# Chunk 1 transposed by a DMA, with the work around it put at other hooks

## The chip, the cores and the metric

The kernel runs on one core of a Trainium2 chip. TensorE (PE) multiplies matrices, VectorE (DVE) and ScalarE (ACT) work elementwise, GpSimd (POOL) does small work and issues transfers, and SyncE (SP) only issues transfers. Each engine runs its own list of instructions in order and waits on semaphores for others. The metric is the device time of one execution in microseconds; lower is better. Before the change the median of five runs is 179.16 us (178.99 to 180.62).

## The reference, cut to what matters

```python
def _A_ref(x, w_r, w_i):                       # x: 1 x 2048 x 512
    X = rfft2(x.astype(float32), axes=(-2, -1))
    X = X * (w_r + 1j * w_i)                   # filter: 2048 x 257
    return irfft2(X, s=(S, D), axes=(-2, -1)).astype(bfloat16)

def _B_ref(x, w_gate, w_up, w_down):           # 512 -> 1792 -> 512
    h = gelu(x @ w_gate) * (x @ w_up)
    return h @ w_down

xn = layernorm(A_x)                            # over the last axis
out = A_x + _A_ref(xn, A_w_r, A_w_i) + _B_ref(xn, B_w_gate, B_w_up, B_w_down)
```

One row-wise normalized input goes to two branches, a two-dimensional Fourier filter and a gated feed-forward, whose results are added to the input. `B_x` is not read.

## The kernel before, in words

The 2048 rows are 16 tiles of 128 rows, taken as four chunks (m or b = 0 to 3) of four tiles. A chunk is normalized (`ln_stat`, `ln_aggr`, `ln_norm`: VectorE, with one reciprocal root on GpSimd) into a buffer `xn` or, for chunk 2, `tw`, and must then be transposed into `xnT`, features on partitions, because TensorE sums over partitions. `trans` does this with eight TensorE transposes into PSUM and one eviction, on VectorE or ScalarE, for half a chunk; `trans_dma` does a whole chunk with one transposing DMA from SyncE's queue. Chunks 0 and 1 use `trans` (chunk 0 partly in a finer form), chunks 2 and 3 `trans_dma`.

**Feed-forward.** For each chunk and each of 14 slices fc of the hidden size, `gate` and `up` are four matmuls each into one PSUM bank; ScalarE takes the gelu of the gate into one of three buffers and VectorE multiplies (L912). The second matmul of a chunk is done by `product`, a Strassen-like scheme: seven steps of seven matmuls for each pair of tiles, with sums of hidden slices (`sum_01`, `sums_S`) and of weights (`sums_T`) made on VectorE. Steps 0 and 3 of a product have ScalarE copy one PSUM bank to another (`copy`, L811); steps 2 and 4 add to those copies. The down weights `wd` come in four loads.

**Fourier branch.** Four stages. `butter` (VectorE, two parts per chunk) folds `xnT`, `unit_D` (one per tile) does the transform over features, `units_A` the first half of the transform over rows, and its result goes to DRAM scratch with `load_tv` reading it back in another order into `tv`. `unit_B` (eight, g = 0 to 7, needing all of `tv`) does the second half; VectorE multiplies by filter slice g (L606, `mul`); `unit_C` begins the inverse and writes to a second scratch, which `load_vv` reads back; `unit_E` and `unit_F` end the inverse and a GpSimd-issued accumulating DMA adds it to the result. The filter arrives in eight slices (`load_W`), each as eight loads: four for the real part by GpSimd's queue, four for the imaginary part by SyncE's, into a ring of four slots. `keep_256` copies a slice's last column, and `mini` (steps 0 to 4) takes that column's own path.

**Order.** It is written out by hand. The main loop runs over chunks b and slices n: `gate`, a hook, sometimes a product step (which has its own hook at its end), `up`, a hook. `hook` has a running number and emits what `at(number, ...)` has planned for it, in the order in which it was planned. So a hook number is a place in TensorE's instruction list, 0.86 us of matmuls or one product step from the next, and at the same time a place in every other engine's list: an operation planned at a hook stands behind all that was emitted before it on its engine. Hooks 0 to 27 lie in chunk 0's loop, from 28 in chunk 1's, from 69 in chunk 2's. `load_late` (L348) also waits until TensorE has reached the place where it was planned. Some work (`mul`, the feed-forward product) is put off to the end of the same hook by `later`.

SyncE's queue is the one the change orders anew: x and weight loads at the start, then scratch writes, transposing DMAs, scratch reads, the imaginary filter loads, and the output. The places are set in L960 to L1024.

Of the kernel before, what the change touches and what calls it, by code (L numbers as in the profile page):

```python
# [214 lines left out]
def bass_parallel_sum__spectral_gfnet__glu_gated_geglu__prompt_kernel(  # L215
# [27 lines left out]
    with ExitStack() as es:  # L243
# [328 lines left out]

        def load_W(s):
            hs = slice(2 * s, 2 * s + 2)
            for k, src in enumerate((A_w_r, A_w_i)):
                v = src.rearrange("(k2 r c h) k -> c k2 r h k", r=2, c=2, h=16)
                for c in range(2):
                    for i in range(2):
                        p0 = 64 * c + 32 * i
                        yield (load_late, W[k][s % 4][p0:p0 + 32, :, :, 0:KW], v[c][:, :, hs, :], [("W", k, s, c, i)], [("Wf", s % 4, k, c, i)], "sp" if k else "pool")  # L580
# [6 lines left out]
        def unit_B(g):  # L587
# [12 lines left out]
            i = g % 2  # L600
# [3 lines left out]
            def mul():  # L604
                for k in range(2):
                    op("dve", lambda e, k=k: e.tensor_tensor(pp[i][k], xc[i], W[k][g % 4][:, :, :, 0:256], ALU.mult),  # L606
                       r=[("xc", i)] + [key for c in range(2) for ii in range(2) for key in (("W", k, g, c, ii), ("Wf", g % 4, k, c, ii))], w=[("pp", i, k)])
# [338 lines left out]
        def at(h, *calls):  # L946
            plan.setdefault(int(h), []).extend(calls)
# [12 lines left out]
        for i in range(4):  # L960
            f0, f1 = (0, 4, 8, 11, 14)[i:i + 2]
            at(10 + 2 * i, (load_late, wd_sb[:, f0:f1, :], wdv[:, f0:f1, :], [("wd", fc) for fc in range(f0, f1)]))
        at(18, (load_late, be[:], c_be.ap(), ["be"]))
        at(19, (load_late, mm[:], c_mm.ap(), ["mm"]))
        for s, h0 in enumerate((30, 37, 49, 54, 61, 66, 70, 75)):
            for i, t in enumerate(load_W(s)):
                at(h0 + i // 2, t)
            at(89 + s // 2 if s > 3 else (47, 48, 57, 58)[s], (keep_256, s))
# [5 lines left out]
        for m in range(1, 4):  # L974
            a = (5, 15, 22)[m - 1]
            n = (10, 20, 27)[m - 1]
            t = (16, 29, 35)[m - 1]
# [5 lines left out]
            if m < 2:  # L983
                at(t, (trans, m, (0, 1), (0, 1, 2, 3)))
                at(t + 1, (trans, m, (2, 3), (0, 1, 2, 3), "act"))
            else:
                at(n + 1, (trans_dma, m))
# [4 lines left out]
        for m in range(4):  # L992
            h = (11, 22, 35, 40)[m]
# [5 lines left out]
            at(h + 8 + (4 if m < 1 else 0), (load_tv, m))  # L999
        for g in range(9):  # L1000
            h = int(59 + 4.6 * g)
# [17 lines left out]
        for k in range(4):  # L1019
            at((40, 43, 45, 47)[k], (sums_T, k))  # L1020
# [126 lines left out]
```

## Time and profile before

| What | Value |
|---|---|
| median of five runs | 179.16 us |
| the profiled execution: its own time, its span | 179.21 us, 177.4 us |
| TensorE busy | 171.9 us (97%) |
| VectorE, ScalarE, GpSimd busy | 132.4, 93.3, 54.8 us |
| granted TensorE clock | full in all slices |
| transfers | 27.89 MB, mean 157 GB/s |
| `gate` and `up` matmuls (L890, L906) | 58.1 and 57.9 us |
| TensorE's transposes of chunk 1 (L422) | two groups of eight, at 24.51 and 25.82 us |

The span is what the profiler recorded, the own time what the device measured; 1.8 us lie outside the span. Times in the text are us from the span's start. Matmuls are pipelined, so a row's length overlaps the next row's start; the distance between starts is what a group costs. Releasers of waits are inferred from semaphores.

### The profile page before, as it was taken

To read this page: it belongs to the slowest core of one execution; us is meant where nothing else is said; L and a number is where in the kernel's file an instruction comes from. 1 tells how busy PE (TensorE), PEld (TensorE's weight loads), DVE (VectorE), ACT (ScalarE), POOL (GpSimd) and SP (SyncE) were. 2 spreads that over 40 slices of the span, in tenths; PEclk is the share of its full clock that TensorE was granted. 3 is DMA by queue.
4 is the path that set the end of the run, shared out by engine and by line. 5 is a ranking of instruction groups with operands and counts; after the bars stand their busy time and mean duration, and the time that the engine had idled before them with its cause. 6 is when DMAs were issued, how large, how long until landed. Compare 5 with 4: busy or idle time off the path is not lost.

```text
span 177.4 us, 3787 instructions
## 1 busy us (share of the span) xinstructions
PE 171.9 (97%) x1394; PEld 107.3 (60%) x1394; DVE 132.4 (75%) x329; ACT 93.3 (53%) x156; POOL 54.8 (31%) x107
## 2 busy tenths in 40 slices
PE   7889999999999999999999999999999999999992
PEld 2477564554566566566565656566767666656881
DVE  2768899986588876867875749897867777897552
ACT  3343447764578523456656665337678576642110
POOL 2210444125041056194880000011544635530000
PEclk9999999999999999999999999999999999999999
DMA  4999999898998579479892204490165736551104
GB/s 118 294 237 308 285 291 307 249 206 222 200 179 164 145 199 220 94 197 209 206 240 49 85 20 122 125 328 25 31 118 106 137 86 118 92 91 30 30 6 118
DMA packets 31059, 27.89 MB, mean 157 GB/s; under 512 B 7120, under 2 KB 27984, under 8 KB 30912
## 3 DMA queue, kind: packets, MB, share of 16 engines
q1 hardware_dynamic: 25936, 19.75, 44.8%
q0 software_dynamic: 4272, 7.24, 19.2%
q10 hardware_dynamic: 832, 0.66, 1.4%
q8 instruction: 11, 0.18, 0.5%
q14 instruction: 8, 0.07, 0.2%
HBM read 18.19 MB, written 6.29 MB: 138 GB/s over the span
## 4 chain that ended last, share of the span: by engine, by line
PE 90%; DMA 4%; SPq 2%; ACT 1%; issue 0%; DVE 0%
PE ps L906 27%; PE ps L890 26%; PE ps L792 24%; DMA wu<-in_B_w_up_dram 4%; SPq L346 2%; PE ps L648 2%; PE ps L846 2%; PE ps L620 2%; PE ps L595 2%; PE ps L495 1%; PE ps L466 1%; PE ps L498 1%; PE ps L467 1%; ACT early L601 1%; PE ps L463 1%; ACT early L625 1%
## 5 line engine op out<-in xcount | busy, mean ns | idle before, releaser
L906 PE MATMUL ps<-xnT,wu 128*128 128x512 f16 (+1 forms) x240 | 57.9, 365 | 0.5 <-DMA wu<-in_B_w_up_dram 0.5
L890 PE MATMUL ps<-xnT,wg 128*128 128x512 f16 (+2 forms) x244 | 58.1, 362 | 0.2 <-DMA wg<-in_B_w_gate_dram 0.2
L912 DVE TENSOR_TENSOR hT<-ps,gl 128x512 bf16<-128x512 f32 (+1 forms) x60 | 39.0, 652 | 21.6 <-PE ps L906 15.4
L894 ACT ACTIVATE gl<-ps 128x512 bf16<-128x512 f32 (+1 forms) x60 | 34.1, 569 | 38.7 <-PE ps L890 37.6
L906 PEld LDWEIGHTS ps<-xnT,wu 128*128 128x128 bf16 x240 | 22.5, 98 | 20.6 <-DMA wu<-in_B_w_up_dram 0.6
L890 PEld LDWEIGHTS ps<-xnT,wg 128*128 128x128 bf16 x244 | 22.8, 98 | 16.0 <-issue 0.8
L349 POOL DMA_DIRECT2D wring<-in_A_w_r_dram x32 | 18.7, 661 | 14.2 <-PE ps L792 4.9
L657 POOL COPY tv<-tv 1x128 bf16<-1x128 bf16 x16 | 5.4, 338 | 40.4 <-ACT tv L655 40.3
L792 PE MATMUL ps<-wd,hT 128*128 128x256 bf16 x112 | 14.4, 273 | 0.0
L872 POOL DMA_DIRECT2D x_sb<-tv x16 | 13.2, 864 | 3.4 <-DVE tv L865 2.4
L606 DVE TENSOR_TENSOR early<-early,wring 128x1024 bf16<-128x1024 f16 x16 | 10.3, 687 | 3.7 <-ACT early L601 3.7
L811 ACT ACTIVATE ps<-ps 128x256 f32<-128x256 f32 x16 | 5.9, 372 | 12.9 <-PE ps L792 12.8
L393 DVE BATCH_NORM_STATS2 st<-x_sb 128x6 f32<-128x512 bf16 x16 | 10.6, 683 | 2.4 <-DMA x_sb<-in_A_x_dram 2.4
L401 POOL TENSOR_TENSOR rstd<-vpe,mhalf 128x4 f32<-128x4 f32 (+2 forms) x6 | 5.0, 836 | 23.5 <-DVE vpe L400 23.5
L792 PEld LDWEIGHTS ps<-wd,hT 128*128 128x128 bf16 x112 | 10.7, 98 | 2.5
L471 ACT ACTIVATE early<-ps 128x512 f16<-128x512 f32 x16 | 9.5, 597 | 4.2 <-PE ps L467 4.2
L852 ACT ACTIVATE tv<-ps 128x512 bf16<-128x512 f32 x16 | 9.5, 595 | 3.6 <-PE ps L846 3.6
L792 PE MATMUL ps<-arena,xnT 128*128 128x256 f16 x91 | 11.4, 273 | 0.0
L655 ACT ACTIVATE tv<-ps 128x512 bf16<-128x512 f32 x16 | 9.5, 595 | 3.2 <-PE ps L648 3.2
L601 ACT ACTIVATE early<-ps 128x1024 f16<-128x1024 f32 x8 | 8.2, 1022 | 4.9 <-PE ps L595 4.3
L792 PEld LDWEIGHTS ps<-arena,xnT 128*128 128x128 f16 x91 | 8.6, 98 | 2.3 <-DVE tw L815 0.3
L675 DVE TENSOR_TENSOR x_sb<-ps,x_sb 128x256 bf16<-128x256 f32 x16 | 6.7, 421 | 3.1 <-PE ps L792 3.0
(119 smaller groups left out, 237.4 us busy)
## 6 DMA issues: line engine op xcount, KB each, us to landing
wring<-in_A_w_r_dram POOLq DMA_DIRECT2D x32, 64.2 KB, 5.0
wring<-in_A_w_i_dram SPq DMA_DIRECT2D x32, 64.2 KB, 4.9
tv<-scr SPq DMA_DIRECT2D x8, 256.0 KB, 4.0
scr<-early SPq DMA_DIRECT2D x8, 256.0 KB, 3.0
wring<-scr SPq DMA_DIRECT2D x4, 512.0 KB, 6.0
x_sb<-tv POOLq DMA_DIRECT2D x16, 128.0 KB, 2.7
scr<-early SPq DMA_DIRECT2D x15, 128.0 KB, 3.6
out_dram<-x_sb SPq DMA_DIRECT2D x28, 64.0 KB, 2.1
```

The lines of the kernel that those rows point to most:

```text
L349: op(eng, lambda e: e.dma_start(dst, src), w=list(keys) + list(also), dma=True, after=[("pe", pr.cnt["pe"])])
L393: op("dve", lambda e: e.bn_stats(st[:, j, :], x_sb[:, j, :]), r=[("x", j, 0), ("x", j, 1)], w=[("st", j)])
L471: op("act", lambda e: e.activation(x4.rearrange("p (a c r) -> p a c r", a=2, r=4), bank(bk).rearrange("p (a r c) -> p a c r", a=2, r=4), A ...
L601: op("act", lambda e: e.activation(xc[i].rearrange("p r hh c -> p (r hh c)"), pair(bk), ACT.Copy, scale=SC_B), r=[("ps", bk), ("ps", bk + ...
L606: op("dve", lambda e, k=k: e.tensor_tensor(pp[i][k], xc[i], W[k][g % 4][:, :, :, 0:256], ALU.mult), r=[("xc", i)] + [key for c in range(2) ...
L655: op("act", lambda e: e.activation(z, bank(bk).rearrange("p (a c) -> p a c", a=4), ACT.Copy, scale=SC_E), r=[("ps", bk)], w=[zk] + (TVK if ...
L792: ins = e.matmul(o, st_(f), mv(f), start=(f == 0 and step in (0, 5)), stop=(f == 6), skip_group_check=True)
L872: op("pool", lambda e: e.dma_start(x_sb[:, j, :], ys, accum_op=ALU.add), r=[yk + (0,), yk + (1,), ("x", j, 0), ("x", j, 1)] + acc(j), w=ac ...
L890: ins = e.matmul(bank(bg)[:, c], wg_sb[:, dc, fc * P:(fc + 1) * P], xnT[:, j1:j1 + len(h), dc, :], start=(dc == 0), stop=(dc == 3), skip_g ...
L894: op("act", lambda e: e.activation(gl[k % 3][:, 0:n], bank(bg)[:, 0:n], ACT.Gelu_apprx_tanh), r=[("ps", bg)], w=[("gl", k % 3)])
L906: ins = e.matmul(bank(bu)[:, 0:n], wu_sb[:, dc, fc * P:(fc + 1) * P], xnT[:, j0:j0 + len(jjs), dc, :], start=(dc == 0), stop=(dc == 3))
L912: op("dve", lambda e: e.tensor_tensor(hT[b % 2][:, fc, h0:h0 + n], bank(bu)[:, 0:n], gl[k % 3][:, 0:n], ALU.mult), r=[("ps", bu), ("gl", k ...
```

## The change

Chunk 1 is transposed by `trans_dma`, at hook 11, instead of by two `trans` groups at hooks 16 and 17; its butterflies, `unit_D` and `units_A` stand three hooks later. The four loads of `wd` go from GpSimd's queue at hooks 10 to 16 to SyncE's at 13 to 16. `units_A` of chunks 1, 2 and 3 go to hooks 30, 38 and 44 (from 27, 40 and 45), the scratch reads of chunks 1 to 3 to 33, 45 and 47 (from 30, 43 and 48). Filter loads, `keep_256`, `unit_B`, `unit_C` and one `sums_T` get other hooks. `load_slice` only asserts while the program is built that a ring slot's earlier slice has been multiplied.

```diff
@@ -570,6 +570,12 @@
                 op("act", lambda e: e.activation(row[:], bank(bk)[96:128, 0:64], ACT.Copy, scale=SC_E), r=[("ps", bk)], w=["row"])
                 dma("sp", z256[0:1, :].rearrange("o (r q) -> o r q", q=64), row[:], r=["row"], w=["z256"] + TVK)
 
+        multiplied = set()
+
+        def load_slice(s, *t):
+            assert s < 4 or s - 4 in multiplied
+            t[0](*t[1:])
+
         def load_W(s):
             hs = slice(2 * s, 2 * s + 2)
             for k, src in enumerate((A_w_r, A_w_i)):
@@ -602,6 +608,7 @@
                r=[("ps", bk), ("ps", bk + 1)], w=[("xc", i)] + (EKEYS if g == 0 else []))
 
             def mul():
+                multiplied.add(g)
                 for k in range(2):
                     op("dve", lambda e, k=k: e.tensor_tensor(pp[i][k], xc[i], W[k][g % 4][:, :, :, 0:256], ALU.mult),
                        r=[("xc", i)] + [key for c in range(2) for ii in range(2) for key in (("W", k, g, c, ii), ("Wf", g % 4, k, c, ii))], w=[("pp", i, k)])
@@ -959,13 +966,13 @@
 
         for i in range(4):
             f0, f1 = (0, 4, 8, 11, 14)[i:i + 2]
-            at(10 + 2 * i, (load_late, wd_sb[:, f0:f1, :], wdv[:, f0:f1, :], [("wd", fc) for fc in range(f0, f1)]))
+            at(13 + i, (load_late, wd_sb[:, f0:f1, :], wdv[:, f0:f1, :], [("wd", fc) for fc in range(f0, f1)], (), "sp"))
         at(18, (load_late, be[:], c_be.ap(), ["be"]))
         at(19, (load_late, mm[:], c_mm.ap(), ["mm"]))
-        for s, h0 in enumerate((30, 37, 49, 54, 61, 66, 70, 75)):
+        for s, h0 in enumerate((31, 35, 50, 54, 63, 67, 72, 76)):
             for i, t in enumerate(load_W(s)):
-                at(h0 + i // 2, t)
-            at(89 + s // 2 if s > 3 else (47, 48, 57, 58)[s], (keep_256, s))
+                at(h0 + i // 2, (load_slice, s) + t)
+            at(89 + s // 2 if s > 3 else (46, 48, 60, 64)[s], (keep_256, s))
         cmv = c_cm.ap().rearrange("p (h r c) -> p h r c", h=NJ, r=2)
         for i, h0 in enumerate((54, 57, 63, 68)):
             hs = slice(4 * i, 4 * i + 4)
@@ -974,31 +981,27 @@
         for m in range(1, 4):
             a = (5, 15, 22)[m - 1]
             n = (10, 20, 27)[m - 1]
-            t = (16, 29, 35)[m - 1]
+            t = (19, 28, 35)[m - 1]
             for i in range(4):
                 at(a + i, (ln_stat, 4 * m + i))
             at(a + 3, (ln_aggr, 4 * m, 4))
             for i in range(4):
                 at(n + i // 2, (ln_norm, 4 * m + i))
-            if m < 2:
-                at(t, (trans, m, (0, 1), (0, 1, 2, 3)))
-                at(t + 1, (trans, m, (2, 3), (0, 1, 2, 3), "act"))
-            else:
-                at(n + 1, (trans_dma, m))
+            at(n + 1, (trans_dma, m))
             at(t + 2, (butter, m, 0))
             at(t + 3, (butter, m, 1))
         at(3, (butter, 0, 0))
         at(4, (butter, 0, 1))
         for m in range(4):
-            h = (11, 22, 35, 40)[m]
+            h = (11, 25, 33, 39)[m]
             for i in range(4):
                 at(h + i + (i if m < 1 else 0), (unit_D, 4 * m + i))
             at(h + 5 + (4 if m < 1 else 0), (units_A, m))
             if m == 3:
                 at(h + 7, (mini, 0))
-            at(h + 8 + (4 if m < 1 else 0), (load_tv, m))
+            at((23, 33, 45, 47)[m], (load_tv, m))
         for g in range(9):
-            h = int(59 + 4.6 * g)
+            h = int(60 + 4.5 * g)
             if g < 8:
                 at(h, (unit_B, g))
             if g > 0:
@@ -1017,7 +1020,7 @@
         for k in range(3):
             at((38, 39, 40)[k], (sum_01, 0, 0, k))
         for k in range(4):
-            at((40, 43, 45, 47)[k], (sums_T, k))
+            at((40, 43, 45, 46)[k], (sums_T, k))
         for k in range(4):
             at((101, 101, 102, 103)[k], (sums_S, 2, 0, 4, (k,)))
             at((106, 106, 107, 107)[k], (sums_S, 2, 4, 6, (k,)))
```

## The prediction, made before the changed kernel was run

> **What bounds the kernel now.** I read the page first: busy shares, then the chain that ended last.
>
> ```profile
> PE 171.9 (97%) x1394; PEld 107.3 (60%) x1394; DVE 132.4 (75%) x329; ACT 93.3 (53%) x156; POOL 54.8 (31%) x107
> ...
> PE 90%; DMA 4%; SPq 2%; ACT 1%; issue 0%; DVE 0%
> ```
>
> TensorE is busy 97% of the span, and the chain is TensorE's own work from 11.8 us (the first `up` of chunk 0, held by a weight load) to 174.2 us. So TensorE's instruction list is the time: an instruction removed there is worth its spacing, and a new wait there costs its length. Next, TensorE's rows in order of time where the change removes work:
>
> ```profile
> 23.65 1.03 PE L890 MATMUL ps<-xnT,wg 128*128 128x512 f16 x4
> 24.51 0.61 PE L422 MATMUL ps<-ident,cmx 128*128 128x128 f16 x8
> 24.96 1.03 PE L906 MATMUL ps<-xnT,wu 128*128 128x512 f16 x4
> 25.82 0.61 PE L422 MATMUL ps<-ident,cmx 128*128 128x128 f16 x8
> 26.27 0.22 PE L463 MATMUL ps<-fd,arena 128*128 128x128 f16 x1
> ```
>
> Columns are start, length, engine, line, operation. The next instruction starts 0.45 us after each transpose group (24.96 - 24.51, 26.27 - 25.82), with no gap on either side: this is bound work. Then the chain between 70 and 80 us, for the one place after 12 us where it leaves TensorE:
>
> ```profile
> 74.88 1.02 ACT early L601
> 75.91 0.92 ACT early L625
> 76.82 0.29 ACT ps L811
> ...
> 77.16 0.94 PE ps L792 x7
> ```
>
> The `gate` group that starts at 75.98 lasts 0.86, so TensorE is free at 76.84 and starts at 77.16: 0.32 us lost. ScalarE must evict B(1) and C(0) before it does the copy of a product's step 3, on which step 4 waits. Last, the transfers: SyncE's issues in order of time, and the landing of transposes and of the last x load.
>
> ```profile
> 14.05 4.44 SPq L346 DMA_DIRECT2D x_sb<-in_A_x_dram  x2
> 30.98 4.24 SPq L346 DMA_DIRECT2D scr<-early  x4
> 35.27 2.69 SPq L436 DMA_TRANSPOSE xnT<-tw  x1
> ```
> ```profile
> x_sb<-in_A_x_dram SPq DMA_DIRECT2D x2, 256.0 KB, 13.0
> ```
> ```profile
> xnT<-tw SPq DMA_TRANSPOSE x1, 4.5
> xnT<-cmx SPq DMA_TRANSPOSE x1, 7.6
> ```
>
> SyncE issues nothing from 18.5 to 30.98 us. The last x load, issued at 16.8, lands at 29.8 (13.0 us). A chunk's transpose (16 blocks, 512 KB) holds SyncE 2.5 to 2.7 us and lands 4.5 or 7.6 us after its issue starts.
>
> **The change, part by part.**
>
> *Transposes of chunk 1.* Two groups of eight go: -2 x 0.45 = -0.90 us on the bound. Their evictions go too (VectorE 0.69 us at 25.16, ScalarE 1.02 us at 26.47); neither held TensorE, so they count nothing, but VectorE, full from 22 to 34 us, gets 0.69 us of air.
>
> *The transpose DMA in their place.* Its source is ready when ln_norm of chunk 1 ends on VectorE at 23.3 (22.57 + 0.72), and SyncE is idle then: issue 23.3 to 25.9. First reader is butter(1,0), moved from hook 18 to hook 21; after it comes butter(1,1) at 22, then unit_D(4) on TensorE at hook 25 instead of 22. With the two butterflies later, VectorE reaches hook 21 as follows: reciprocal root of chunk 2 on GpSimd about 28 to 29, two norms 29.0 to 29.7, the product of `up` 10 (whose matmuls end at 31.3 - 0.9) 30.4 to 31.0. butter(1,0) 31.0 to 32.3, two norms to 33.0, butter(1,1) to 33.7. TensorE reaches hook 25 at: end of `gate` 11 now 32.0, less 0.90, plus three groups of 0.86 = 33.7. So unit_D(4) is held about max(0, L - 31.0), L the landing. Lower end: 23.3 + 4.5 = 27.8, no wait. Upper ends: queued behind the x loads landing at 29.8, plus the 1.8 us that the transpose issued at 35.27 took from the end of its issue (37.96) to landing (39.8): 31.6, a wait of 0.6; with the other transpose's 5.1 us (44.6 to 49.7): 34.9, a wait of 3.9. The x loads share the transfer engines now with filter-down weights issued from 21.1, which go behind the transpose, so they should land near 27 (an estimate: 1 MB of the queue's loads were out at 24.1, at the 350 GB/s of 20 to 24 us). Then L is 27 + 1.8 = 28.8 or 27 + 5.1 = 32.1, and the first is the nearer: there too loads drained ahead of the transpose, while the 7.6 us one had 512 KB of scratch reads issued right behind it. I take 0.05 us for the hold; both ends, 0 and 3.9, are kept. A wait there queues VectorE's norms of chunk 2 and the `up` products behind butter(1,0), and after them TensorE.
>
> The Trainium skill, page "VectorE: DVE Perf Modes", section "Rules for kernel authors", speaks against the change: a 128x128 transpose belongs on TensorE where a PSUM destination will do, and its table of transpose paths gives 1309 ns by DMA against 390 ns. By that page 16 blocks in a row would be an estimated 20.9 us, chunk 1 would land near 44, and the kernel would take some 12 us longer. The two transposes in this trace contradict that figure, and on TensorE a block costs 0.45/8 us, not 390 ns.
>
> *Weights of the last product.* Four loads go from GpSimd's queue to SyncE's, at hooks 13 to 16, behind the transpose. Four issues of 0.43 to 0.6 us (rows of the same sizes) end near 28.3; the next in the queue, scratch writes of chunk 0, come ready near 30. GpSimd loses 3.1 us of issuing and nobody waits for it. First use is at 52.7; landings of 10 us put them near 38. Nothing. If the queue backs up as at 14.05 (4.44 us for two issues), the scratch writes start up to about 3 us late, and chunk 2's transpose (now 35.27, landing 39.8) with them; unit_D(8) comes at hook 33, near 43 by the same counting, so that still costs 0 to 0.5. I take 0.
>
> *Scratch, chunks 2 and 3.* units_A go to hooks 20, 30, 38, 44 (from 20, 27, 40, 45), reads of the scratch to 23, 33, 45, 47. Today the last read is issued at 64.7 and 65.3 and lands near 69.6; unit_B(0) starts at 70.61, 1.0 us of cover. Afterwards units_A(3) is a hook earlier, so the last read is issued near 63 and lands by 68; unit_B(0), a hook later but with 0.9 removed, stays at 70.6. Gain 0 (TensorE doesn't wait today); if the cover is gone, chunk 2's writes behind slice 1 on SyncE being late, some 1 us. I take 0.
>
> *Filter slices.* All 64 loads remain, moved by -2 to +2 hooks past scratch operations. SyncE's eight of slices 0 and 1 now stand around the read of chunk 1, which waits for its writes, so slice 1 comes some us later, near 60; its multiplication is at hook 64, near 73. Slices 4 to 7 keep about 11 to 15 hooks (0.86 us or more each) before use, against 5 us to land. On GpSimd the small copies of column 256 of slices 2 and 3 go from hooks 57, 58 to 60, 64; today they block it 3.65 us at 70 to 73.7 with constants behind them. Nothing on TensorE; were a slice late, VectorE's L606 would wait and unit_C after it.
>
> *Backward units.* unit_B(1) and unit_C(0) go from hook 63 to 64, behind the product step that emits the copy. ScalarE then does the copy first and the 0.32 us goes. Between 0 and -0.32; I take -0.32, since all other steps 0 and 3 of products keep two or more TensorE groups between the copy and its use with no eviction of B and C before it. What is late next is the `gelu` of the following gate, which has a ring of three buffers.
>
> *Small column path.* mini(2) and unit_C(7) move from hook 95 to 96, mini(3) stays at 98. It keeps two groups, 1.72 us, instead of product plus two groups. VectorE's work between (product sum 0.65, add 0.42, four small ones 0.7) ends within 0.1 of TensorE's arrival. Ends 0 and 0.65 (the sum if it comes in between); I take 0.1. The reads of the inverse's scratch (issued 111.72, landing 116.7, first use 118.05, cover 1.35) lose one product (0.77) and gain back part as their chain also starts earlier: cover about 1. Nothing.
>
> **Sum** against the profiled execution, 179.21 (177.4 span and 1.8 outside): -0.90 - 0.32 + 0.05 + 0.10 = -1.07, 178.14. The median of the runs is 179.16, 0.05 less, so 178.1.
>
> **Rivals.** What measurement can tell from no change is 0.5%, 0.90 us, so 178.26 and 180.06 are the bounds.
>
> *A smaller gain (within 0.5%).* The 0.32 us comes back at another eviction, or unit_D(4) waits to the middle end, L = 31.6. Time 179.16 - 0.90 + 0.15 = 178.4 for the one, 179.16 - 1.12 + 0.6 = 178.6 for the other. For it: my count of VectorE has no slack at hook 22 to 25. Against: products elsewhere in the trace wait nowhere on the copy.
>
> *Slower: transpose late.* It sits behind x loads in SyncE's queue and shares with weights behind it, as the 7.6 us one shared with scratch reads. unit_D(4) waits L - 31.0 on TensorE; faster turns to no change near L = 31.2, and no change to slower at L = 33.0. At 34.9 the time is 179.16 - 1.12 + 3.9 = 181.9. For it: transfer engines are full from 4.4 to 35 us; against: less stands ahead of it than today at the same moment.
>
> *The transpose gain is not there.* If TensorE was not the bound at 24 to 27 us, the 0.90 would reappear as a wait before hook 30, and the time would be 179.16 - 0.32 + 0.15 = 179.0. Against: no idle time on TensorE between 12 and 77 us beyond changes of tile shape.
>
> **How the numbers follow.** As summed: 0.57, own range 177.8 to 178.3. Smaller gain: 0.21. Transpose gain absent: 0.08. Late transpose, or a wait of its size on another transfer: 0.14. Faster 0.57, same 0.29, slower 0.14. The range goes from 177.7 (178.1 less the spread of 0.2 below the median before, and the 0.15 of waits gone) to 179.8, which holds all but the slower case and a little.
>
> **What would show it.** Right: no transpose group between 24 and 27 us; unit_D(4) near 33.7 right after its `up`; TensorE's idle time at 77 gone; last add near 173.1 instead of 174.2. Wrong: VectorE idle before butter(1,0) with the transpose as releaser, a gap before unit_D(4), 5, or SyncE issuing scratch writes later than 31; gaps at unit_B(0), at mini(3) near 109, or at a product's step 4.

## The result, and the profile after

| | Before | Changed |
|---|---|---|
| median of all runs on the chip | 179.58 us (45 runs, 178.89 to 181.12) | 181.01 us (26 runs, 179.07 to 183.33) |
| ratio to before, 95% interval | 1 | 1.0049 (1.0028 to 1.0069) |
| the profiled execution: its own time, its span | 179.21, 177.4 us | 180.05, 178.1 us |
| TensorE busy | 171.9 us | 172.1 us |

The change was forecast to save 1.07 us and costs about 0.49% of 179.6, 0.9 us: just at the size that can be told from no change, with an interval that lies wholly on the slow side. 181.01 is outside the range on record, and by the two medians of all runs the cost is 1.43 us. (The ratios leave out executions more than 1.5% above the fastest of their kernel; the profiles of e2, e7, e12 and e15 are of such executions and are used only to see where TensorE waits.)

In the code of the changed kernel the lines have moved down by seven: L897 is `gate`, L913 `up`, L799 a product step, L601 `unit_B`, L607 its eviction, L613 the multiplication by a filter slice, L761 a sum of weights, L818 the copy and L822 the sum in the product's steps. The butterflies (L446 to L450), the matmuls of `unit_D` (L463 to L467) and the transposing DMA (L436) keep their numbers.

The page of the changed kernel, busy shares and chain. The sixteen transposes are gone from TensorE's count (1394 to 1378), and less of the chain is TensorE's own work: its share fell from 90% to 85%, and VectorE and ScalarE, 1% together before, have 6%.

```profile
PE 172.1 (97%) x1378; PEld 106.5 (60%) x1378; DVE 131.3 (74%) x328; ACT 92.4 (52%) x155; POOL 51.9 (29%) x103
...
PE 85%; DVE 4%; DMA 4%; SPq 2%; ACT 2%; issue 1%; DVEq 0%
```

TensorE's rows in order of time, at the five places that matter (start, length, engine, line, operation; idle time and its releaser in brackets).

```profile
24.66 1.03 PE L913 MATMUL ps<-xnT,wu 128*128 128x512 f16 x4
25.52 0.22 PE L463 MATMUL ps<-fd,arena 128*128 128x128 f16 x1
...
32.98 1.03 PE L913 MATMUL ps<-xnT,wu 128*128 128x512 f16 x4
33.85 0.23 PE L463 MATMUL ps<-fd,arena 128*128 128x128 f16 x1
...
42.31 1.03 PE L913 MATMUL ps<-xnT,wu 128*128 128x512 f16 x4
44.20 0.23 PE L463 MATMUL ps<-fd,arena 128*128 128x128 f16 x1 [0.86 <-DVE arena L450]
...
62.70 1.03 PE L897 MATMUL ps<-xnT,wg 128*128 128x512 f16 x4
63.83 0.94 PE L799 MATMUL ps<-arena,hT 128*128 128x256 f16 x7
...
74.07 1.03 PE L913 MATMUL ps<-xnT,wu 128*128 128x512 f16 x4
75.28 0.94 PE L799 MATMUL ps<-arena,xnT 128*128 128x256 f16 x7 [0.19 <-DVE tw L822]
...
76.93 1.04 PE L897 MATMUL ps<-xnT,wg 128*128 128x512 f16 x4
77.81 0.93 PE L799 MATMUL ps<-arena,hT 128*128 128x256 f16 x7
```

A group of four 512-wide matmuls costs 0.86 us from start to start. By that: no transposes stand at 25 us any more; `unit_D(4)` starts at 33.85, 0.01 late; `unit_D(8)` at 44.20 is 44.20 - 42.31 - 0.86 = 1.03 late; the product step at 63.83 is 0.27 late, the one at 75.28 0.35 late; the old loss of 0.32 at 77 is gone (77.81 - 76.93 = 0.88). These are all the losses after 13 us.

**A balance.** The early loads of weights hold TensorE for a time that differs by over 2 us between the profiles here, whose kernels are alike up to there (the first full group starts at 15.5 us in e2 and at 17.9 in e15), so I compare from the start of the first full `gate` group (128x512, four matmuls) of chunk 0 to the start of the last add, and call it the body. Before: 15.75 to 174.22, 158.47 us. Changed: 15.90 to 174.89, 158.99 us. From the parts: 158.47 - 0.90 (transposes) - 0.32 (the wait at 77) + 1.03 + 0.27 + 0.35 = 158.90, 0.09 from what was measured. So both gains that were forecast are there, and three waits took them back.

**Why `unit_D(8)` is late.** SyncE's issues in order of time, changed kernel (start, length of issuing):

```profile
13.66 5.35 SPq L346 DMA_DIRECT2D x_sb<-in_A_x_dram  x2
23.36 4.87 SPq L436 DMA_TRANSPOSE xnT<-cmx  x1
28.27 2.21 SPq L349 DMA_DIRECT2D wd<-in_B_w_down_dram  x4
30.52 3.05 SPq L346 DMA_DIRECT2D scr<-early  x4
33.61 5.99 SPq L436 DMA_TRANSPOSE xnT<-tw  x1
39.93 1.18 SPq L346 DMA_DIRECT2D tv<-scr  x2
41.16 3.73 SPq L436 DMA_TRANSPOSE xnT<-cmx  x1
```

The queue, idle from 18.5 to 31 us before, is now busy almost without a break from 23.4 to 45 us. Chunk 2's transpose starts its issue 1.7 us earlier than before (33.61 against 35.27), but the issue takes 5.99 us instead of 2.69. Its landing, from the transfers by issue (us from the start of the issue): 7.9 instead of 4.5, so chunk 2 lands at 41.5 instead of 39.8.

```profile
xnT<-cmx SPq DMA_TRANSPOSE x1, 7.2
...
xnT<-tw SPq DMA_TRANSPOSE x1, 7.9
```

TensorE comes to `unit_D(8)` at 43.17, where it came at 45.63 before:

```profile
45.63 0.22 PE L463 MATMUL ps<-fd,arena 128*128 128x128 f16 x1
```

That is two hooks (the diff moves the unit from hook 35 to 33, and its butterflies by one) and the 0.90 earlier. VectorE's rows show what lies between the landing and the matmul: the butterflies, a feed-forward product among them, 2.6 us in all.

```profile
41.58 0.69 DVE L446 TENSOR_TENSOR cmx<-xnT 128x1024 f16<-128x1024 f16 x1 [0.59 <-DMA xnT<-tw]
42.19 0.69 DVE L447 TENSOR_TENSOR arena<-xnT 128x1024 f16<-128x1024 f16 x1
42.79 0.69 DVE L919 TENSOR_TENSOR hT<-ps,gl 128x512 bf16<-128x512 f32 x1
43.39 0.42 DVE L449 TENSOR_TENSOR arena<-cmx 128x512 f16<-128x512 f16 x1
43.72 0.42 DVE L450 TENSOR_TENSOR arena<-cmx 128x512 f16<-128x512 f16 x1
```

**Why the two product steps are late.** VectorE's and ScalarE's rows in front of them. Before, near 58 us:

```profile
57.99 0.69 DVE L912 TENSOR_TENSOR hT<-ps,gl 128x512 bf16<-128x512 f32 x1 [0.63 <-PE ps L906]
58.98 1.09 DVE L754 TENSOR_TENSOR arena<-wd 128x1792 f16<-128x1792 bf16 x1 [0.29 <-PE ps L498]
```

Changed, near 60 and near 74 us:

```profile
59.40 0.69 DVE L919 TENSOR_TENSOR hT<-ps,gl 128x512 bf16<-128x512 f32 x1 [1.39 <-PE ps L913]
60.01 1.08 DVE L761 TENSOR_TENSOR arena<-wd 128x1792 f16<-128x1792 bf16 x1
...
62.73 1.05 DVE L761 TENSOR_TENSOR arena<-wd,arena 128x1792 f16<-128x1792 bf16 x1
...
72.54 1.02 ACT L607 ACTIVATE early<-ps 128x1024 f16<-128x1024 f32 x1 [1.39 <-PE ps L538]
...
73.60 1.29 DVE L613 TENSOR_TENSOR early<-early,wring 128x1024 bf16<-128x1024 f16 x2 [0.63 <-ACT early L607]
74.81 0.42 DVE L822 TENSOR_TENSOR tw<-ps,x_sb 128x256 f32<-128x256 f32 x1
```

At 63.83 it is VectorE's list: the third sum of weights started at 60.01, where before it started at 58.98. Before, the `up` group came first, its feed-forward product (57.99) was made early, and the sum started as soon as `units_A(3)`, behind that group, had finished. Now `units_A(3)` comes a hook earlier, the `up` group follows it, and the sum stands behind that group's product (59.40). The list is then full up to the fourth sum (62.73), for which the step waits. At 75.28 it is `unit_B(0)`, a hook later by its number: ScalarE's eviction (72.54) and VectorE's multiplication by slice 0 (1.29 us for its two parts, 73.60 to 74.89) now stand ahead of the sum (74.81) on which the next product step waits.

### The profile page after: what moved, and what is told of

The parts are those of the page before. It is cut to its first block, busy times and chain, and to the rows that moved or that the text cites. A ratio compares the mean times of both kernels' runs of the same rounds, so it can differ in the third digit from the quotient of the medians.

```text
span 178.1 us, 3757 instructions
## 1 busy us (share of the span) xinstructions
PE 172.1 (97%) x1378; PEld 106.5 (60%) x1378; DVE 131.3 (74%) x328; ACT 92.4 (52%) x155; POOL 51.9 (29%) x103
## 3 DMA queue, kind: packets, MB, share of 16 engines
q0 software_dynamic: 3760, 5.40, 15.6%
## 4 chain that ended last, share of the span: by engine, by line
PE 85%; DVE 4%; DMA 4%; SPq 2%; ACT 2%; issue 1%; DVEq 0%
PE ps L913 25%; PE ps L897 25%; PE ps L799 23%; DMA wu<-in_B_w_up_dram 4%; SPq L346 2%; PE ps L627 2%; PE ps L655 2%; PE ps L853 2%; PE ps L601 2%; DVE arena L761 1%; ACT early L505 1%; PE ps L466 1%; PE ps L467 1%; PE ps L495 1%; PE ps L498 1%
## 5 line engine op out<-in xcount | busy, mean ns | idle before, releaser
L897 PE MATMUL ps<-xnT,wg 128*128 128x512 f16 (+2 forms) x244 | 58.1, 362 | 0.2 <-ACT xnT L1044 0.2
L913 PE MATMUL ps<-xnT,wu 128*128 128x512 f16 (+1 forms) x240 | 57.9, 365 | 0.2 <-DMA wu<-in_B_w_up_dram 0.2
L913 PEld LDWEIGHTS ps<-xnT,wu 128*128 128x128 bf16 x240 | 22.4, 98 | 20.6 <-issue 1.4
L897 PEld LDWEIGHTS ps<-xnT,wg 128*128 128x128 bf16 x244 | 22.6, 98 | 16.2 <-issue 0.8
L349 POOL DMA_DIRECT2D wring<-in_A_w_r_dram x32 | 18.5, 620 | 15.4 <-PE ps L897 6.1
L799 PE MATMUL ps<-wd,hT 128*128 128x256 bf16 x112 | 14.4, 273 | 0.0
L818 ACT ACTIVATE ps<-ps 128x256 f32<-128x256 f32 x16 | 5.9, 368 | 13.7 <-PE ps L799 13.5
L799 PEld LDWEIGHTS ps<-wd,hT 128*128 128x128 bf16 x112 | 10.8, 98 | 2.7
L613 DVE TENSOR_TENSOR early<-early,wring 128x1024 bf16<-128x1024 f16 x16 | 10.3, 686 | 2.4 <-ACT early L607 2.4
L799 PE MATMUL ps<-arena,xnT 128*128 128x256 f16 x91 | 11.4, 273 | 0.2 <-DVE tw L822 0.2
L682 DVE TENSOR_TENSOR x_sb<-ps,tw 128x256 bf16<-128x256 f32 x16 | 6.8, 422 | 5.0 <-PE ps L799 4.6
L799 PEld LDWEIGHTS ps<-arena,xnT 128*128 128x128 f16 x91 | 8.7, 98 | 2.7 <-DVE tw L822 0.7
L607 ACT ACTIVATE early<-ps 128x1024 f16<-128x1024 f32 x8 | 8.2, 1021 | 4.2 <-PE ps L601 2.8
```

Of the source, the lines that this page charges most:

```text
L349: op(eng, lambda e: e.dma_start(dst, src), w=list(keys) + list(also), dma=True, after=[("pe", pr.cnt["pe"])])
L799: ins = e.matmul(o, st_(f), mv(f), start=(f == 0 and step in (0, 5)), stop=(f == 6), skip_group_check=True)
L897: ins = e.matmul(bank(bg)[:, c], wg_sb[:, dc, fc * P:(fc + 1) * P], xnT[:, j1:j1 + len(h), dc, :], start=(dc == 0), stop=(dc == 3), skip_g ...
L913: ins = e.matmul(bank(bu)[:, 0:n], wu_sb[:, dc, fc * P:(fc + 1) * P], xnT[:, j0:j0 + len(jjs), dc, :], start=(dc == 0), stop=(dc == 3))
```

## The experiments

They are told in the order of the question that they answer. Where the expectations use letters: Q is the queue (chunk 2's transpose late behind what SyncE now carries), H the hooks (the earlier place of `unit_D(8)` alone), S the sums in front of product steps, L the loads that run beside the first transpose. "Loss" is time lost on TensorE, read as above.

**Is the wait at `unit_D(8)` worth the difference?** e2 puts it two hooks later, the place that it had before, and `units_A(2)` with it.

```diff
-            h = (11, 25, 33, 39)[m]
+            h = (11, 25, 35, 39)[m]
```

> The changed kernel with unit_D(8) to unit_D(11) back at hooks 35 to 38 and units_A(2) at 40; transposes, queues and all else as changed. Theory H: the wait of 1.03 us before unit_D(8) goes, time about 1.0 us below the changed kernel (179.4 against its 180.4 in undisturbed runs). Theory Q expects the wait to go too, since unit_D(8) comes 1.7 us later, but the second transpose to land as late as in the changed kernel, near 41.5. If instead another wait takes its place (tv for unit_B(0), as units_A(2) comes later), unit_B(0) shows a gap and the time stays.

Ratio 0.998 (0.9949 to 1.0011), against 1.0049 (1.0028 to 1.0069) for the changed kernel: the intervals don't meet, and two hooks at one unit are worth some 0.7%, 1.2 us. Its profile is of an execution of 182.10 us; in it `unit_D(8)` still lost 0.43, 1.70 had moved on to `unit_D(12)`, and 1.45 was lost at 120.8. That is more than in the changed kernel, so no trace shows where the other executions save their time.

The changed kernel was also profiled a second time, with a new set of runs.

> The changed kernel again, beside the two that follow. Expected from its own numbers: 0 to 0.7% above the kernel before, with a wait of 0.5 to 1.5 us before unit_D(8) behind the second transpose, issued for 5.5 to 6.5 us.

Ratio 1.0049 (1.0023 to 1.0076). The same two units wait, and longer. TensorE in order of time:

```profile
34.01 0.23 PE L463 MATMUL ps<-fd,arena 128*128 128x128 f16 x1 [0.26 <-DVE arena L450]
...
45.15 0.23 PE L463 MATMUL ps<-fd,arena 128*128 128x128 f16 x1 [1.65 <-DVE arena L450]
```

Losses 0.42 and 1.82, then the same 0.27 and 0.35. Body: 158.47 - 1.22 + 2.86 = 160.11, measured 160.19. So the waits on transfers vary from execution to execution and the two on VectorE's order don't; this also fits the wider spread of the changed kernel's times.

**Queue or hooks?** e11 leaves chunk 1 on TensorE, at its old two hooks, and keeps all the rest of the change.

```diff
-            at(n + 1, (trans_dma, m))
+            if m < 2:
+                at(16, (trans, m, (0, 1), (0, 1, 2, 3)))
+                at(17, (trans, m, (2, 3), (0, 1, 2, 3), "act"))
+            else:
+                at(n + 1, (trans_dma, m))
```

> The changed kernel with chunk 1 transposed on TensorE again, by the two groups at hooks 16 and 17; down weights in SyncE's queue at hooks 13 to 16 and all other hooks as changed. TensorE has 0.90 us more to do. Theory Q (the first transpose pushes the weights, and both push the second transpose): without it the weights are issued near 21 to 24 and drained before chunk 0's scratch writes, the second transpose is issued in under 4 us and unit_D(8) waits under 0.5 us, so the time is within 0.3% of the changed kernel, the 0.90 us being about what the wait costs. If the gain of 0.90 us is real and the other waits stay the same, the time is 0.5% above the changed kernel; if the hooks alone make the wait, the wait stays at 1 us.

Ratio 1.005 (1.0019 to 1.008), the same as with the DMA. Without the first transpose in the queue, chunk 2's transpose issues in 2.37 us and lands 4.6 us after its start, 38.4; `unit_D(8)` loses 0.35 all the same. SyncE's issues and TensorE's row:

```profile
33.83 2.37 SPq L436 DMA_TRANSPOSE xnT<-tw  x1
```
```profile
44.10 0.23 PE L463 MATMUL ps<-fd,arena 128*128 128x128 f16 x1 [0.18 <-DVE arena L450]
```

So of the 1.03, 0.35 is the earlier hook (VectorE has not made the butterflies yet, whatever the landing), and the other 0.68, or 1.47 in the second profile, is the late transpose. The moves of the change alone cost 0.35 + 0.27 + 0.35 - 0.32 = 0.65 (body 158.47 + 0.65 = 159.12, measured 159.21), and the transposing DMA gives back 0.90 and takes a wait of 0.68 to 1.47, plus 0.01 to 0.42 at `unit_D(4)`: by the two ratios, nothing is left of it.

**Is it the down weights in the queue?** e9 keeps them on SyncE but at hook 22, behind chunk 2's transpose; e6 puts them at hook 29, behind all three transposes.

```diff
-            at(13 + i, (load_late, wd_sb[:, f0:f1, :], wdv[:, f0:f1, :], [("wd", fc) for fc in range(f0, f1)], (), "sp"))
+            at(22, (load_late, wd_sb[:, f0:f1, :], wdv[:, f0:f1, :], [("wd", fc) for fc in range(f0, f1)], (), "sp"))
```

> The changed kernel with the four loads of the down weights in SyncE's queue at hook 22, between the second and the third transpose. At hook 29 they freed the second transpose (issue 1.85 us, unit_D(8) waiting 0.18) but held chunk 1's scratch writes (8.9 us to land) and with them every later scratch read, so unit_B(0) waited 7.0 us. Theory Q expects here: second transpose issued in under 3 us, unit_D(8) waits under 0.5 us, the third transpose lands later than 8 us after issue but before its butterflies need it near 50, unit_B(0) does not wait, time 0.3% to 0.6% below the changed kernel. The rival, that the 1.8 MB holds whatever stands behind it in this queue, wherever it is put, expects a wait of over 0.7 us at unit_D(12) or unit_B(0) and no gain.

> The changed kernel with the four loads of the down weights still in SyncE's queue, but at hook 29, behind all three transposes, instead of hooks 13 to 16, behind the first. Theory Q: with nothing but chunk 0's scratch writes ahead of it the second transpose is issued in under 4 us and lands before 39.5; the wait before unit_D(8) falls from 1.0 to at most 0.5 us (VectorE's own butterflies), time 0.3% to 0.6% below the changed kernel. Rival P (a transpose is slow beside any scratch traffic): its issue still takes over 5 us and the time stays. If the weights then come too late, the first weight sums at hook 40 and product steps show gaps near 54.

e9: ratio 1.0051 (1.0021 to 1.008). SyncE's issues:

```profile
34.60 2.04 SPq L436 DMA_TRANSPOSE xnT<-tw  x1
36.69 2.73 SPq L349 DMA_DIRECT2D wd<-in_B_w_down_dram  x4
39.60 1.18 SPq L346 DMA_DIRECT2D tv<-scr  x2
41.87 5.24 SPq L436 DMA_TRANSPOSE xnT<-cmx  x1
```

The transpose ahead of the weights issues fast, and the one behind them (5.24 us, landing 9.4 us after its start) has become the slow one. `unit_D(8)` is down to VectorE's 0.35, `unit_D(12)` loses 0.72 and `unit_B(0)` 0.88; with 0.28 and 0.35 the body is 158.47 - 1.22 + 2.58 = 159.83, measured 159.81. e6: ratio 1.0466 (1.0411 to 1.052). Chunk 2's transpose issues in 1.85 us and `unit_D(8)` loses 0.35 (`unit_D(4)` loses 0.80: the first transpose, with no weights behind it, landed 8.6 us after its start). But what now stands behind the 1.8 MB of weights (two loads of 512 and two of 384 KB) is the scratch of the Fourier branch; its last read comes late enough to stop TensorE for 7 us:

```profile
79.91 0.64 PE L601 MATMUL ps<-tv,be 64*64 64x256 f16 x8 [7.00 <-DMA tv<-scr]
```

Both say the same: the 1.8 MB delay whatever stands next behind them in the queue, and every place tried has something that TensorE needs.

**Why not leave the weights where they were?** e1 puts them back on GpSimd's queue, all else as changed. e4 does the same from the other side: the kernel before with only chunk 1's transpose by DMA, and its butterflies, `unit_D`, `units_A` and scratch read at the changed hooks.

```diff
-            at(13 + i, (load_late, wd_sb[:, f0:f1, :], wdv[:, f0:f1, :], [("wd", fc) for fc in range(f0, f1)], (), "sp"))
+            at(10 + 2 * i, (load_late, wd_sb[:, f0:f1, :], wdv[:, f0:f1, :], [("wd", fc) for fc in range(f0, f1)]))
```

> The changed kernel with the four loads of the down weights back on GpSimd's queue at hooks 10, 12, 14 and 16; all else as changed. Theory Q (queue): the 1.8 MB of weights in SyncE's queue between the first and the second transpose hold up chunk 0's scratch writes (landing 6.6 to 7.3 us after issue, 4.7 to 5.5 before the change) and the second transpose (issue 5.99 us long instead of 2.69, landing at 41.5 instead of 39.8), so unit_D(8) waits 1.03 us; expected here: second transpose lands before 40.5, unit_D(8) waits under 0.5 us, time 0.5 to 1 us below the changed kernel. Theory H (hooks): unit_D(8) stands two hooks earlier than before and VectorE, not the transfer, is what it waits for; expected here: the wait stays above 0.7 us and the time stays within 0.4 us of the changed kernel's. Theory L (load): the same bytes now run beside the x loads again, and the first transpose lands later, so unit_D(4) waits in its place by up to 1 us.

The edit of e4, against the kernel before:

```diff
-            t = (16, 29, 35)[m - 1]
+            t = (19, 29, 35)[m - 1]
...
-            if m < 2:
-                at(t, (trans, m, (0, 1), (0, 1, 2, 3)))
-                at(t + 1, (trans, m, (2, 3), (0, 1, 2, 3), "act"))
-            else:
-                at(n + 1, (trans_dma, m))
+            at(n + 1, (trans_dma, m))
...
-            h = (11, 22, 35, 40)[m]
+            h = (11, 25, 35, 40)[m]
...
-            at(h + 8 + (4 if m < 1 else 0), (load_tv, m))
+            at((23, 33, 43, 48)[m], (load_tv, m))
```

> The kernel before with only chunk 1's transpose by DMA at hook 11, its butterflies at 21 and 22, unit_D(4) to (7) at 25 to 28, units_A(1) at 30 and its scratch read at 33; the weights stay on GpSimd's queue and everything else at its old hook. If the two transpose groups are worth their 0.90 us on TensorE and the damage comes from the rest of the change: 0.6 to 0.9 us below the kernel before, no wait above 0.3 us at unit_D(4) or unit_D(8). If the transfer itself is the damage: unit_D(4) or unit_D(8) waits by 0.5 to 1.5 us and the time is not below the kernel before.

e1: ratio 1.052 (1.0468 to 1.0572); e4: 1.0465 (1.0414 to 1.0516). My expectations were of a wait of a microsecond or so, and missed by far. e1's transfer of chunk 1, and VectorE's and TensorE's rows that wait for it:

```profile
xnT<-cmx SPq DMA_TRANSPOSE x1, 16.6
```
```profile
40.62 0.69 DVE L446 TENSOR_TENSOR cmx<-xnT 128x1024 f16<-128x1024 f16 x1 [8.80 <-DMA xnT<-cmx]
```
```profile
43.30 0.29 PE L463 MATMUL ps<-fd,arena 128*128 128x128 f16 x1 [8.75 <-DVE arena L450]
```

The transpose takes 16.6 us instead of 7.2 (15.6 in e4) when the weights come from another queue at the same time, and `unit_D(4)` loses 8.92 (7.96 in e4). Chunk 2's transpose, 9 us later and with the weights out of SyncE's queue, issues in 1.82 us and lands in 5.6. So the place of the weights on SyncE behind the first transpose isn't a side matter: it keeps them out of that transpose's way, as the later places of e6, e8, e9 and e10 do, where it landed in 5.6 to 8.6 us. Two things change together here: GpSimd issues the first weights at 21.8 us, ahead of the transpose (24.0), where SyncE issues them at 28.3, behind it. No run has another queue's weights behind the transpose, so how much is the queue and how much the earlier issue is not shown. e7 asks whether this is GpSimd's queue or any other, with the weights on ScalarE's.

```diff
-            at(13 + i, (load_late, wd_sb[:, f0:f1, :], wdv[:, f0:f1, :], [("wd", fc) for fc in range(f0, f1)], (), "sp"))
+            at(10 + 2 * i, (load_late, wd_sb[:, f0:f1, :], wdv[:, f0:f1, :], [("wd", fc) for fc in range(f0, f1)], (), "act"))
```

> The changed kernel with the four loads of the down weights at hooks 10, 12, 14 and 16 as in the kernel before, but issued from ScalarE's queue. With them on GpSimd's queue the first transpose took 16.6 us to land and the kernel 9 us longer. Theory R (rings): what slows a transpose is any other queue's descriptors taken in turn with its own; expected: first transpose lands 12 to 17 us after issue, unit_D(4) waits 4 to 9 us, time 184 to 189. Theory G (GpSimd): it is the software queue that does it; expected: lands within 9 us, time within 1.5 us of the changed kernel.

Ratio 1.0528 (1.0485 to 1.057); the first transpose lands 18.3 us after its start, and `unit_D(4)` loses 7.89, after 0.84 and 1.80 lost on late `gate` and `up` weights. So it is not GpSimd's queue alone.

**The two product steps.** e3 puts `unit_B`, `unit_C` and the small column's steps back.

```diff
-            h = int(60 + 4.5 * g)
+            h = int(59 + 4.6 * g)
```

> The changed kernel with unit_B, unit_C and the small column's steps back at the hooks of before (59 plus 4.6 for each g); all else as changed. Theory S (order on VectorE): at hook 60 the filter product of unit_B(0) stands ahead of the sum on which a product's step 3 waits (0.35 us lost before 75.28), while at hook 63 the evictions stand ahead of a copy (0.32 us lost before 77.16 in the kernel before); expected here: the first gap goes and the second comes back, time within 0.2 us of the changed kernel. Rival: the two gaps are independent of these hooks; expected: both or neither change, time different by over 0.3 us.

The 0.35 at 75 is gone and the old wait is back, in its old form:

```profile
77.55 0.94 PE L799 MATMUL ps<-arena,hT 128*128 128x256 f16 x7 [0.15 <-ACT ps L818]
```

It lost 0.32 there, 0.27 at 63.6, and 0.70 and 0.33 at `unit_D(8)` and `unit_D(12)`; body 158.93. The ratio, 0.9998 (0.9964 to 1.0032), overlaps that of the changed kernel, so from the times this exchange can't be told; from the trace it is 0.35 for 0.32. Two versions then mend both steps and `unit_D(8)` by moving `unit_B(0)` alone back to 59, the third sum of weights from hook 45 to 44 and `unit_D(8)` to 34; e8 with the weights at hook 29, e10 with them at 22.

```diff
-            h = (11, 25, 33, 39)[m]
+            h = (11, 25, 34, 39)[m]
...
-            h = int(60 + 4.5 * g)
+            h = int(60 + 4.5 * g) if g else 59
...
-            at((40, 43, 45, 46)[k], (sums_T, k))
+            at((40, 43, 44, 46)[k], (sums_T, k))
```

> The changed kernel with four repairs: down weights at hook 29 in SyncE's queue, unit_D(8) to (11) at hooks 34 to 37, unit_B(0) at hook 59 while the others keep theirs, and the third weight sum at hook 44. Theories Q and S together expect the waits before unit_D(8) (1.03), at 63.8 (0.27) and at 75.3 (0.35) to go: 1.3 to 1.6 us below the changed kernel, 0.4% to 0.7% below the kernel before. The rival, that transposes by DMA give back what they save wherever the queue stands, expects a new wait of over 0.5 us and a time within 0.3% of the kernel before.

> As the one before, and unit_D(8) to (11) at hooks 34 to 37, unit_B(0) at hook 59 with the others as changed, the third weight sum at hook 44. Theories Q and S together: waits before unit_D(8) (1.03), at 63.8 (0.27) and at 75.3 (0.35) all go, 0.4% to 0.7% below the kernel before. The rival expects a wait of over 0.7 us in their place and a time within 0.3% of the kernel before or above it.

e8: 1.055 (1.0504 to 1.0596), e10: 1.0058 (1.0025 to 1.0091). In both the losses at `unit_D(8)`, 63.8, 75.3 and 77 us are gone: the causes named for the two steps hold. Neither is faster, because the weights' place costs more: e8 loses 6.73 at `unit_B(0)` and 0.72 at the product step at 56.03, and e10 loses 1.38 and 1.21 at the two places next behind them. TensorE in e10:

```profile
51.83 0.23 PE L463 MATMUL ps<-fd,arena 128*128 128x128 f16 x1 [1.20 <-DVE arena L450]
...
72.07 0.41 PE L601 MATMUL ps<-tv,be 64*64 64x256 f16 x8 [1.04 <-DMA tv<-scr]
```

Splitting the weights doesn't help either: e12 is e8 with two of the four loads at hooks 13 and 14 and two at 29.

```diff
+            at((13, 14, 29, 29)[i], (load_late, wd_sb[:, f0:f1, :], wdv[:, f0:f1, :], [("wd", fc) for fc in range(f0, f1)], (), "sp"))
```

> The changed kernel with the first two loads of the down weights at hooks 13 and 14 and the last two at hook 29, all in SyncE's queue, and unit_D(8) to (11) at hooks 34 to 37, unit_B(0) at 59, the third weight sum at hook 44. If the waits come from how many bytes stand ahead of each transfer: second transpose issued in under 5 us, no wait above 0.4 us at unit_D(8), unit_D(12) and unit_B(0), 0.3% to 0.6% below the kernel before. If the queue has no slack anywhere: a wait of 0.7 us or more at one of the three places and a time from 0.2% below to 0.5% above the kernel before.

Ratio 1.0092 (1.0052 to 1.0131), with `unit_B(0)` waiting again (3.82 in its profile). Chunk 2's transpose, behind two of the loads instead of four, issued there in 2.03 us, and nothing was lost at `unit_D(8)`.

**What the moved backward units give by themselves.** e13 and e14 take the kernel before and move `unit_B` and `unit_C` from the second on (hooks 64 to 96), so that the copy comes before their evictions. e14 also issues filter slice 6 a hook later, and has the changed kernel's assertion on the slices' order; e13 leaves the slices alone.

```diff
-        for s, h0 in enumerate((30, 37, 49, 54, 61, 66, 70, 75)):
+        for s, h0 in enumerate((30, 37, 49, 54, 61, 66, 71, 75)):
...
-            h = int(59 + 4.6 * g)
+            h = int(60 + 4.5 * g) if g else 59
```

> The kernel before with only unit_B(1) to (7), unit_C and the small column's steps at the changed kernel's hooks (64, 69, 73, 78, 82, 87, 91, 96); unit_B(0) stays at 59. Theory S: the 0.32 us lost before 77.16 goes and nothing takes its place: 0.1% to 0.25% below the kernel before. Rival: the eviction's place shifts a wait to another product step, time unchanged within 0.05%.

> The kernel before with unit_B(1) to (7), unit_C and the small column's steps at the changed kernel's hooks and slice 6 loaded from hook 71 instead of 70, so that it stands behind slice 2's multiplication. Theory S: the 0.32 us before 77.16 goes and nothing takes its place, 0.1% to 0.25% below the kernel before. Rival: a wait shifts to another place, time unchanged within 0.05% or above.

e13: 1.0423 (1.0374 to 1.0472). In it the multiplication by slice 2 is emitted at the end of hook 70, behind the first loads of slice 6 into the same ring slot, so it uses part of slice 6 in place of slice 2 and waits for it. That is a 6.42 us loss before `unit_C` at 91.75; the change has slice 6 at hook 72. e14: 1.0027 (0.9988 to 1.0066). Its body is 158.26, 0.21 below before, and TensorE loses nothing after 14 us. ScalarE in order of time, the copy now ahead of both evictions:

```profile
77.04 0.37 ACT L818 ACTIVATE ps<-ps 128x256 f32<-128x256 f32 x1 [1.13 <-PE ps L799]
77.40 1.02 ACT L607 ACTIVATE early<-ps 128x1024 f16<-128x1024 f32 x1
78.32 1.02 ACT L632 ACTIVATE early<-ps 128x1024 bf16<-128x1024 f32 x1
```

So the 0.32 is real as a wait removed, and too small for these runs to show as a time: that execution lost 1.81 to an early weight load, and the interval holds 1.

**The smallest form of the change.** e15 is e14 with chunk 1's transpose by DMA (as in e4) and the weights on SyncE behind it at hooks 13 to 16; the units of chunks 2 and 3 keep their old hooks.

```diff
-            at(10 + 2 * i, (load_late, wd_sb[:, f0:f1, :], wdv[:, f0:f1, :], [("wd", fc) for fc in range(f0, f1)]))
+            at(13 + i, (load_late, wd_sb[:, f0:f1, :], wdv[:, f0:f1, :], [("wd", fc) for fc in range(f0, f1)], (), "sp"))
```

> The same, and chunk 1 transposed by DMA as in the change, with the down weights behind it in SyncE's queue at hooks 13 to 16, unit_D(4) to (7) at 25 to 28, units_A(1) at 30, its scratch read at 33; the units of chunks 2 and 3 at the hooks of before (35 and 40, units_A 40 and 45). If it is only the earlier hooks of chunks 2 and 3 that turn the later transposes into waits: waits before unit_D(8) and unit_D(12) under 0.4 us, 0.3% to 0.6% below the kernel before. If the queue is too full wherever the units stand: a wait of 0.7 us or more at unit_D(12) or at unit_B(0), whose scratch read now comes after the same writes but 0.9 us of TensorE's work earlier, and a time within 0.3% of the kernel before or above.

Ratio 0.9964 (0.9917 to 1.0012), the lowest of all, with an interval that still holds 1. But it stands on the six shortest of 14 executions; all 14 spread from 178.61 to 186.89, and their median is 181.74, against 179.71 for the kernel before. In its profile chunk 2's transpose is as slow to issue as in the changed kernel (5.65 us), `unit_D(8)` at its old place doesn't care, and the losses are 0.64 at `unit_D(12)` and 3.19 at `unit_B(0)`, behind the scratch. No version here is shown to be faster than the kernel before.

## Why the prediction was wrong, point by point

- *What bounds the kernel*: right. Every loss and gain on TensorE shows in the end to within 0.1 us of body in the four full-clock balances above.
- *Transposes of chunk 1*, -0.90: right; 24.66 to 25.52 is one group's spacing with nothing between.
- *The transpose DMA in their place*, 0.05 at `unit_D(4)`: 0.01 and 0.42 in two profiles, inside its ends (0.80 in e6). The landing was put at 28.8, or 32.1 for the slower row; it was 30.6, 7.2 us after a start at 23.36; the last x load, put near 27, came at 28.5 (17.39 + 11.1). (In the kernel before it landed at 29.3, not 29.8: the 13.0 us is the median of two loads.) But the reason given is wrong: loads that share the engines were costed as if they only drained ahead. e1, e4 and e7 measured 15.6 to 18.3 us with the weights on another queue, a price far outside both ends, 4.5 and 7.6, and the change avoids it because the weights go behind, in the same queue.
- *Weights of the last product*: this is the step that failed. It took 0 and kept 0 to 0.5 for `unit_D(8)`, from a delay of the scratch writes. The scratch writes did start on time (30.52); what was mis-sized is the transpose behind them, whose issue was taken as 2.69 us and was 5.99. And the place was checked against a landing alone, not against landing plus the 2.6 us of VectorE's list before the matmul. The wait was 1.03 and 1.82.
- *Scratch, chunks 2 and 3* and *Filter slices*, 0: right in the changed kernel, no loss at `unit_B(0)` nor behind a filter slice. How thin the first cover is, e6, e8, e9, e10 and e15 showed: 0.88 to 7.17 lost there when the queue carries the same bytes in another order. What no step costed is the third sum of weights, which the earlier `units_A(3)` put behind an `up` group's product: 0.27.
- *Backward units*, -0.32: right for the wait it named. "All other steps keep two or more groups" counted ScalarE's evictions alone; VectorE's multiplication, put ahead of a product's sum by the same move, cost 0.35. Net +0.03 for this step.
- *Small column path*, +0.10: no loss to speak of at `mini(3)`, 0.1 too much.

The sum should have been -0.90 - 0.32 + (1.03 to 1.82) + (0.01 to 0.42) + 0.27 + 0.35 = +0.4 to +1.6, and the runs' 0.9, or 1.43 by the medians, lies inside. Of the 2.9 us between 178.1 and 181.0, another 0.4 is the base: the kernel before has a median of 179.58 over 45 runs, not the 179.16 of five.

The rival "Slower: transpose late" had the right kind of mechanism on the wrong transpose: it looked at the first, which has little ahead of it, while the one behind it inherits a full queue. The rival that the transpose gain is absent is refuted by the balance, though e11 shows that in time it comes to that. The rule weighed against the change, from the Trainium skill, "VectorE: DVE Perf Modes", section "Rules for kernel authors", with the figures of its section "The three transpose paths" (1309 ns for a 128x128 block by DMA, against 390 by TensorE), gave an estimated 20.9 us a chunk. In the changed kernel a chunk took 7.2 to 8.3 us, 0.45 to 0.52 a block; with the weights on another queue the first took 15.6 to 18.3, 0.98 to 1.14 a block. So the figure was too high for the change as made and not far off for e1, e4 and e7, and the page's advice, to stay on TensorE, turned out no worse here, for another reason.

## What to carry to other kernels

An operation taken off the bound engine and put on a queue pays through what stands behind it in that queue: cost the next two or three entries with the queue full, not with the durations of the idle queue. Every in-order list past a moved item has to be walked, VectorE's as well as the evicting engine's, and a cover is counted from the landing plus the work that stands between landing and use. Where an execution's start varies more than the effect, a balance of losses between two fixed points in the trace tells what the times can't.

## What the runs showed of the hardware that was not expected

- A 512 KB transposing DMA from SyncE landed 7.2 us after its start with the weights behind it in its own queue, and 15.6 (e4), 16.6 (e1) and 18.3 us (e7) with the same weights on GpSimd's or ScalarE's, the first of them issued 2 to 5 us before it. That the two streams share something is shown; what they share, and how much the earlier issue counts, is not.
- The time that SyncE's queue needs to issue such a transpose is no constant: 1.6 to 2.7 us in the kernel before and for chunks 2 and 3 in e1, e6, e7, e8 and e11; 3.5 to 6.6 us for all three in the changed kernel, e2, e3 and e5; and 6.6 (e4), 8.1 (e1) and 11.0 (e7) for the first one with the weights on another queue.
- A long wait on TensorE costs more than its length. In e1 TensorE started again at 43.3 us, and stretches of the trace show the granted clock (third column from the end) at half until 48 us:

```profile
44.00:46.00 2.00, 2.00 (x8) 0.88 (x7) 2.00 (x4) 0.74 (x2) 0.00 (x0) 0.50 1.58 145
...
48.00:50.00 2.00, 2.00 (x16) 1.24 (x15) 1.79 (x5) 1.17 (x3) 0.42 (x1) 0.97 0.60 131
```

Its body is 169.24, and 158.47 - 1.22 + 8.92 + 0.27 + 0.37 = 166.81: the other 2.43 us agree with about 4.8 us at half rate. e4 and e6, with waits of 8.0 and 7.2, have 2.0 and 1.6 us more than their losses. The trace's own records of the clock give 0.50 from 37.87 to 48.11 us in e1, which is 10.24 us, and for 6.83 us each in e4 and e6. The Trainium skill, "TensorE: Matmul & The Clock Gate", section "Part 1: The HAM clock gate", describes such a gate, half rate after idle time, with a window of about 3.4 us; the trace agrees, in the 0.50 and in these lengths, three and two times 3.41. Waits of 1 to 2 us (the changed kernel's own) and the 3.19 of e15 kept the full clock. In e12 the 3.82 at `unit_B(0)` did not, and neither did three waits of 0.8 to 1.1 us one after the other near its start, which were followed by 3.41 us at 0.50 from 14.71 us on.
